# Attention groups in twos: the last score of one group beside the first score of the next

## The chip, the cores and the metric

The kernel runs on one core of one Trainium2 chip. The metric is the device time of one execution in microseconds, the median of several runs. The engines that matter here are TensorE (PE, matrix multiplication), ScalarE (ACT, activations such as the exponential), VectorE (DVE, reductions) and GpSimd (POOL); SyncE (SP) issues the DMAs.

## The reference

One transformer block without learned norm weights, on 2048 rows of 512 numbers:

```python
h = x + _A_ref(_layernorm(x), wqkv, wo)       # S = 2048, D = 512
h2 = h + _B_ref(_layernorm(h), w1, w2)        # F = 1792

def _A_ref(x, wqkv, wo):                      # 32 heads of 16 columns
    q, k, v = ...                             # x @ wqkv, split by head
    scores = jnp.einsum("bhqd,bhkd->bhqk", q, k) * Dh ** -0.5
    p = _softmax(scores, axis=-1)
    return einsum("bhqk,bhkd->bhqd", p, v) (heads joined) @ wo

def _B_ref(x, w1, w2):
    return silu(x @ w1) @ w2
```

## The kernel before, in words

The kernel projects queries, keys and values first (until about 190 us of the span). Then comes attention, with the output projection and the MLP of each block of 512 rows put in as soon as the heads of that block are done.

Attention is cut into 32 items (`ITEMS`). An item is four heads by 512 query rows. Each item is cut into 16 groups (`KC`), one for each 128 keys, so there are 512 groups. A group `g` has four scores, numbered `k` = 0 to 3, one for each head (in the last item, two heads by two chunks of keys). For each score, `scores(g, k)` (L414) does one matmul of the keys with the queries into a PSUM bank (`ps_s`, 128 keys by 512 queries, recorded at L96 as all matmuls) and one exponential on ACT from that bank into an SBUF tile (`pt`, L110). Two groups later, `values(g - LAG)` (L749, `LAG` is 2) multiplies the four `pt` with the values into one bank (`pv`, eight recorded matmuls).

The softmax needs each query's largest score ahead of time, since the negative maximum is part of the operands (extra rows of `qs` and `ks`). So each item's maxima are found some items earlier: `one_max` (L358) calls `maximum` (L259), one matmul of queries with keys into a bank (`ps_m`) and one reduction on DVE (`mx`, L271). There are 64 for each item. `maxima(g)` (L1154) plans how many of them (0 to 3, mostly 3) go into a group. When an item's maxima are complete, `place_max` transposes them and sends them to the operands by DMA.

The operands of a score take 64 rows and those of a maximum 48, so one of each fits on the array at a time, if they lie in different halves of the rows. `HEADS` gives each score number its pair `(a, j)`, and `j` is the half: scores 0 and 2 of a group are in half 1, scores 1 and 3 in half 0 (in the last item 0 and 2 in half 0). `one_max` is called with the other half, `1 - j`, so that the maximum can stand beside the score just issued.

The order on each engine is the order in which the program issues, written out by hand: matmuls, activations, reductions and DMAs are kept in program order. Behind the scores and maxima of a group come the placing of finished maxima, in a few groups the output projection (`output`), and then the values of two groups before.

During attention the eight PSUM banks are given out by

```python
open_banks(ctx, 2, st=4, m0=1, m1=1, pv=1, m2=1)
```

Scores take the four `st` banks in turn, as do the output projections; maxima take `m0`, `m1` and `m2` in turn; `pv` is one bank. A tile in a bank can be written only after the readers of the tile that had the bank before are done.

Three groups (`marks`: 144, 272, 400) begin with an MLP block; the scores of such a group and of the next are issued inside the MLP ahead of time, as those of groups 0 and 1 are beside the last projections. Those groups have no maxima. The last twelve groups (500 to 511) have none either, since all 2048 are found by then.

Of the kernel before, what the change touches and what calls it, by code (L numbers as in the profile page):

```python
# [88 lines left out]
def attention_mlp_kernel(ctx: ExitStack, tc: tile.TileContext, x, wqkv, wo, w1, w2, out):  # L89
# [58 lines left out]
    def bank(name, kind="st", dtype=F32):  # L148
        pool_of = banks[kind]
        if isinstance(pool_of, list):  # L150
            pool_of.append(pool_of.pop(0))
            return pool_of[-1].tile([P, 512], dtype, tag=pool_of[-1].name, name=name)
        return pool_of.tile([P, 512], dtype, tag=kind, name=name)
# [88 lines left out]
    def head(g, k):  # L242

        i, c = divmod(g, KC)
        if i < LAST:
            return *HEADS[k], c
        return c // HALF, k % 2, c % HALF * 2 + k // 2

    def piece_of(i, a):

        return i, a if i == LAST else None
# [7 lines left out]
    def maximum(i, kb, qt, a, j, ps=None):  # L259

        piece = piece_of(i, a)
        n = 1 if i == LAST else 2
        if piece not in mx:
            mx[piece] = small.tile([P, 64], F32, name="mx", bufs=RING + 1)[:, :32 * n].rearrange(
                "p (j a q k) -> p j a q k", j=2, a=n, k=4)
            left[piece] = 32 * n
        if ps is None:
            ps = bank("ps_m", "sm")
        mm(ps, qs[i % RING][64 * j:64 * j + 48, a, qt * P:qt * P + P],
           ks[i % RING][64 * j:64 * j + 48, a, kb * 512:kb * 512 + 512], start=True, stop=True)  # L270
        pin(nc.vector.tensor_reduce(mx[piece][:, j, a % n, qt, kb:kb + 1], ps, axis=AX.X, op=ALU.max))  # L271
        left[piece] -= 1
        return left[piece] == 0

    def finish_max(piece, urgent):

        m4 = mx.pop(piece).rearrange("p j a q k -> p (j a q) k")
        rows = m4.shape[1]
        nm = small.tile([P, 16], F32, name="nm")[:, :rows]
        sign = 1.0  # L280
        if urgent:
            pin(nc.vector.tensor_reduce(nm, m4, axis=AX.X, op=ALU.max, negate=True))  # L282
        else:
            sign = -1.0
            m1, m2 = m4[:, :, :2], m4[:, :, 2:]
            for to, a, b in ((m2, m1, m2), (nm, m2[:, :, 0], m2[:, :, 1])):

                pool("tensor_tensor", to, b, a, ALU.subtract)
                pool("tensor_scalar", to, to, 0.0, None, op0=ALU.max)
                pool("tensor_tensor", to, to, a, ALU.add)  # L290
        ns = small.tile([P, 32], F16, name="ns")[:, :2 * rows]
        high, rest = (ns.rearrange("p (j r a) -> p j r a", j=2, r=2)[:, :, r, :] for r in range(2))
        nm = nm.rearrange("p (j a) -> p j a", j=2)
        pool("tensor_scalar", nm, nm, sign / MX, None, op0=ALU.mult)
        pool("tensor_copy", high, nm)
        pool("tensor_tensor", rest, nm, high, ALU.subtract)
        split[piece] = ns
# [3 lines left out]
    def finish_rest():  # L301
        while unfinished:
            finish_max(unfinished.pop(), True)
# [27 lines left out]
    def soon(steps, fn, *a):  # L331

        agenda.setdefault(at["step"] + steps, []).append((fn, a))
# [11 lines left out]
    def next_item():  # L345
        while at["item"] < ITEMS and not (todo[at["item"], 0] or todo[at["item"], 1]):
            at["item"] += 1
        return at["item"]

    def due_at(piece):  # L350

        g = at["group"]
        if g is None:
            return WAIT + 1
        joint = g + WAIT + (JOINT - g - WAIT) % KC
        return joint - g if joint < start_of(piece) - 2 and joint // KC - 1 not in (-1, *FIRSTS) else WAIT

    def one_max(half=None, ps=None):  # L358

        i = next_item()  # L360
        if i == ITEMS:
            return
        if half is None:
            half = at["half"]
            at["half"] = 1 - half
        if at["blocks"]:

            i = min(range(2), key=lambda n: (todo[n, half] or todo[n, 1 - half] or [(n, KC)])[0][1])
        elif not todo[i, half] and 64 * (i + 2) <= at["ready"] and KC * i - at["next"] > 12:

            i += 1
        half = half if todo[i, half] else 1 - half
        at["done"] += 1
        block = todo[i, half].pop(0)
        piece = piece_of(i, block[3])
        found_all = maximum(*block, ps)

        finish_rest()
        if found_all:
            steps = due_at(piece)  # L380
            g = at["group"]
            if g is None or g + 1 in marks:
                soon(steps, place_max, piece)
                finish_max(piece, g is not None)
                return
            late.setdefault(at["step"] + steps, []).append(piece)
            if steps == WAIT:
                unfinished.append(piece)
                found_at["step"] = at["step"]
            else:  # L390
                finish_max(piece, False)
# [15 lines left out]
    pts, den, pools = {}, {}, []  # L407
# [6 lines left out]
    def scores(g, k, kind="st"):  # L414

        i = g // KC
        a, j, c = head(g, k)
        assert piece_of(i, a) in placed
        ps = bank("ps_s", kind)
        mm(ps, ks[i % RING][64 * j:64 * j + 64, a, c * P:(c + 1) * P], qs[i % RING][64 * j:64 * j + 64, a, :],  # L420
           start=True, stop=True)
        pts[g, k] = pt_tile("pt")
        act("activation", pts[g, k], ps, AF.Exp, scale=qk_f)


    with ExitStack() as pa:
# [289 lines left out]
        for g in range(1, NG // 2):  # L716
            for m, (b, key) in enumerate([(b, 1) for b in range(NB)] + [(b, 0) for b in range(NB)]):
# [3 lines left out]
                n = 8 * g + m - 12  # L721
# [5 lines left out]
                beside = {BESIDE_A1[m]: 6} if g == 1 and m < len(BESIDE_A1) else BESIDE_A  # L727
                if n >= 18:
                    beside = BESIDE_T[n - 18]
# [446 lines left out]
    for g in range(groups):  # L1176
        tick()
        i, c = divmod(g, KC)
        at["group"], at["next"] = None, g
        if g in marks:  # L1180
            finish_block(i // 8 - 1, (g - 2, g - 1))
        if i + RING - 1 < ITEMS and 6 <= c < 14:
            (load_k if c % 2 else load_q)(i + RING - 1, c // 2 - 3)
        if g < DC:
            w = raw_tile()
            dma(w, wo[g * P:(g + 1) * P, :])
            soon(8, split_wo, g, w)
        f, c4 = divmod(g - SPLIT, 4)
        if c4 == 0 and 0 <= f < 2 * FC:
            kind, f = ("w1", "w2")[f % 2], f // 2  # L1190
            soon(4, split_weights, kind, f, load_raw(kind, f))
        if i in FIRSTS:
            b, n = i // 8 - 1, c - OUTPUT
            if c < 4:
                load_rows(b, c)
            if c in first_weights:
                load_weights(*first_weights[c])
            if c in (3, 4):

                split_rows(b, c - 3, slice(0, DC - 1))  # L1200
            if n == 0:
                for t in range(2):
                    split_rows(b, t, slice(DC - 1, DC))
        if i == LAST:
            if c < 4:
                load_rows(NB - 1, c)
            if 5 <= c < 9:

                split_early(c - 5)
            if c == 4:  # L1210
                for f in range(3):
                    load_weights("w1", f)
                load_weights("w2", 0)
        if g == 1:
            dve("memset", pv, 0.0)
        at["group"] = g
        n = maxima(g)

        half = 1 - head(g, g % 2)[1]
        j = next_item()  # L1220
        more = len(todo[j, half]) - len(todo[j, 1 - half]) if j < ITEMS else 0
        beside = range(n)
        if n == 3 and more < 0:
            beside = range(1, 4)
        if n == 2 and more > 0:
            beside = 0, 2
        for m in range(4):
            k = m ^ (g % 2)
            if (g, k) not in pts:
                scores(g, k)  # L1230
            if m in beside:
                one_max(1 - head(g, k)[1])
        if found_at["step"] < at["step"]:
            finish_rest()
        for j in late.pop(at["step"], ()):

            place_max(j)
        if i in FIRSTS and OUTPUT + 1 < c < OUTPUT + 4:

            split_rows(i // 8 - 1, c - OUTPUT)  # L1240
        if i in FIRSTS and c > OUTPUT:
            output(i // 8 - 1, c - OUTPUT - 1)
        if g - LAG >= 0 and not (g in marks or g - 1 in marks):
            values(g - LAG)
# [34 lines left out]
```

## Time and profile before

| | |
|---|---|
| median of 3 runs | 1631.33 us (1630.3 to 1633.35) |
| the profiled execution | 1629.9 us, its span 1628.1 us |
| granted TensorE clock | 0.997 of full speed |
| PE, DVE, ACT busy | 1609.1, 1408.7, 1207.2 us |
| exponentials of scores on ACT | 2048, 1010.5 us |
| reductions of maxima on DVE | 1971 from ps_m, 1232.9 us, and 77 from pv, 52.9 us |

Rows of the timeline have the start, the duration, the engine, the line, the operation, what it writes and reads, and how many instructions are merged; in brackets is the idle time of the engine ahead of it and what ended it. PE durations are modelled: matmuls overlap, so the distance between two starts says more than a duration. The chain of work is followed back from the last instruction, in each step to what released it; "issue" is time in which the engine waited for nothing that the profile shows. A row of the waits has the total idle time in us, how often, and the longest.

### The profile page before, as it was taken

What the parts mean: (1) busy time and instruction counts of PE and PEld (TensorE: products, weight loads), DVE (VectorE), ACT (ScalarE), POOL (GpSimd) and SP (SyncE); (2) the same over time, 40 slices, a digit from 0 to 9 for tenths busy, and PEclk for the clock granted to TensorE, in tenths of its full rate; (3) what the DMA queues carried; (4) which work ended last, traced back from release to release, by engine and by line L of the source; (5) the groups of instructions that cost most, each with busy time, mean ns of one, the idle gap of its engine ahead of it and who ended that gap; (6) DMA issues with size and microseconds to landing.
All of it is one profiled execution on the core that took longest, in us unless ns stands there. A gap on an engine that the chain in (4) does not pass through costs nothing.

```text
span 1628.1 us, 28586 instructions
## 1 busy us (share of the span) xinstructions
PE 1609.1 (99%) x10553; PEld 518.3 (32%) x10553; DVE 1408.7 (87%) x2340; ACT 1207.2 (74%) x2391; POOL 443.7 (27%) x696
## 2 busy tenths in 40 slices
PE   9899999999999999999999999999999999999998
PEld 7566522222223322222223322222223322222254
DVE  7799999999998889999998889999986789998431
ACT  5445599999974249999974249999974179999732
POOL 4323454534524301121225201121126201111100
PEclk9999999999999999999999999999999999999999
DMA  5657343433432211111232211112133211100222
GB/s 194 172 143 220 102 96 113 114 98 107 118 90 69 88 51 32 33 37 46 58 77 86 72 51 33 33 37 53 52 78 95 62 51 34 35 12 22 72 85 71
DMA packets 100952, 125.91 MB, mean 77 GB/s; under 512 B 24144, under 2 KB 61072, under 8 KB 100812
## 3 DMA queue, kind: packets, MB, share of 16 engines
q1 hardware_dynamic: 100812, 124.10, 27.4%
q8 instruction: 82, 1.34, 0.3%
q14 instruction: 58, 0.48, 0.1%
HBM read 93.45 MB, written 24.63 MB: 73 GB/s over the span
## 4 chain that ended last, share of the span: by engine, by line
PE 88%; DVE 6%; ACT 4%; DMA 1%; issue 1%; POOL 0%; SPq 0%; DVEq 0%; ACTq 0%
PE pv L96 30%; PE ps_s L96 22%; PE ps_m L96 9%; PE ps_acc L96 9%; PE ps_w L96 8%; PE ps_qk L96 5%; DVE mx L271 4%; ACT pt L110 3%; PE ps_wo L96 2%; PE ps_v L96 2%; DMA ks<-in_B_w_dram 1%; PE ps_tr L99 1%; DVE st L113 0%; PE ps_n L99 0%; DVE ot L113 0%
## 5 line engine op out<-in xcount | busy, mean ns | idle before, releaser
L271 DVE TENSOR_REDUCE mx<-ps_m 128x1 f32<-128x512 f32 x1971 | 1232.9, 682 | 53.8 <-PE ps_m L96 23.3
L110 ACT ACTIVATE pt<-ps_s 128x512 f32<-128x512 f32 x2048 | 1010.5, 609 | 152.2 <-PE ps_s L96 133.0
L96 PE MATMUL pv<-pt,va 128*17 128x512 f32 x4096 | 537.5, 598 | 0.6
L96 PE MATMUL ps_s<-qs,ks 64*128 64x512 f16 x2048 | 532.5, 379 | 2.3 <-ACT pt L110 0.5
L96 PE MATMUL ps_m<-ks,qs 48*128 48x512 f16 x1971 | 499.3, 380 | 5.5 <-DVE mx L271 5.2
L96 PEld LDWEIGHTS <-ks 64*128 64x128 f16 x2048 | 149.8, 95 | 548.5 <-issue 434.7
L103 POOL TENSOR_TENSOR ri<-rc,minus 128x16 f32<-128x16 f32 x31 | 90.7, 2927 | 261.5 <-DMA rc<-dn 261.5
L96 PE MATMUL ps_acc<-w,gh 128*128 128x512 f16 x672 | 157.2, 380 | 0.0
L96 PEld LDWEIGHTS <-qs 48*128 48x128 f16 x2048 | 119.0, 94 | 65.0 <-issue 54.5
L96 PEld LDWEIGHTS pv<-pt,va 128*17 128x17 f32 x4096 | 68.9, 95 | 215.9 <-issue 203.7
L110 ACT ACTIVATE g<-ps_w,factors 128x512 f32<-128x512 f32 x56 | 38.5, 687 | 127.6 <-PE ps_w L96 123.3
L96 PE MATMUL ps_w<-hth,w 128*128 128x512 f16 (+1 forms) x472 | 132.9, 369 | 0.0
L96 PEld LDWEIGHTS <-w 128*128 128x128 f16 x708 | 66.1, 98 | 87.9 <-issue 20.8
L96 PEld LDWEIGHTS <-gh 128*128 128x128 f16 x672 | 61.1, 98 | 90.9 <-issue 25.0
L271 DVE TENSOR_REDUCE mx<-pv 128x1 f32<-128x512 f32 x77 | 52.9, 687 | 42.6 <-PE ps_m L96 41.2
L103 POOL TENSOR_TENSOR mx<-mx 128x32 f32<-128x32 f32 x40 | 9.6, 241 | 284.9 <-DVE mx L271 283.2
L96 PE MATMUL ps_w<-htl,w 128*128 128x512 f16 (+1 forms) x236 | 83.9, 368 | 0.0
L103 POOL TENSOR_SCALAR nm<-nm 128x16 f32<-128x16 f32 (+1 forms) x53 | 13.5, 254 | 176.2 <-DVE nm L282 148.7
L110 ACT ACTIVATE ks<-ps_qk,qk_s 128x512 f32<-128x512 f32 x30 | 20.7, 688 | 53.2 <-PE ps_qk L96 45.7
L113 DVE SCALAR_TENSOR_TENSOR gh<-g,factors,gh 128x512 f16<-128x512 f32 x14 | 10.5, 752 | 52.1 <-ACT gh L110 52.1
L103 POOL TENSOR_TENSOR sl<-ks,sh 128x512 f16<-128x512 f32 x30 | 34.8, 1161 | 70.4 <-ACT sh L110 57.0
L96 PE MATMUL ps_qk<-xth,wqk_h 128*128 128x512 f32 x128 | 53.6, 419 | 0.4 <-ACT va L110 0.4
(133 smaller groups left out, 1046.5 us busy)
## 6 DMA issues: line engine op xcount, KB each, us to landing
ks<-kd SPq DMA_DIRECT2D x120, 192.0 KB
w<-w1d SPq DMA_DIRECT2D x56, 256.0 KB
w<-w2d SPq DMA_DIRECT2D x56, 256.0 KB
ks<-in_B_w_dram SPq DMA_DIRECT2D x28, 256.0 KB
w<-in_B_w_dram SPq DMA_DIRECT2D x28, 256.0 KB
qs<-qd SPq DMA_DIRECT2D x128, 48.0 KB
kd<-sh SPq DMA_DIRECT2D x16, 256.0 KB
qd<-sh SPq DMA_DIRECT2D x16, 256.0 KB
```

The lines of the kernel that those rows point to most:

```text
L96: tc.keep_in_program_order(nc.tensor.matmul(*a, **k))
L99: tc.keep_in_program_order(nc.tensor.transpose(*a))
L103: tc.keep_in_program_order(getattr(nc.gpsimd, op)(*a, **k))
L110: pin(getattr(nc.scalar, fn)(*a, **k))
L113: pin(getattr(nc.vector, fn)(*a, **k))
L271: pin(nc.vector.tensor_reduce(mx[piece][:, j, a % n, qt, kb:kb + 1], ps, axis=AX.X, op=ALU.max))
```

## The change

Groups are taken in twos. In an even group `g` the loop goes over five scores, the four of `g` and then score 0 of group `g + 1`. In an odd group it goes over the other three, 1, 2 and 3. Before, an odd group took its four in the order 1, 0, 3, 2. Each score may have a maximum behind it, as before; with three maxima in an even group these go behind its first three scores, so that the fourth score (half 0) has the fifth (half 1) as its neighbour. In an odd group each of its three scores has a maximum. The number of maxima planned for each group is the same. The rule that shifted three maxima to the last three scores when the halves were unevenly used up is gone. The values of two groups before still come at the end of each group, so in an even group they now stand behind five scores.

```diff
-        half = 1 - head(g, g % 2)[1]
+        if g % 2:
+            slots = [(g, k) for k in (1, 2, 3)]
+        else:
+            slots = [(g, k) for k in range(4)] + [(g + 1, 0)]
+        half = 1 - head(*slots[0])[1]
         j = next_item()
         more = len(todo[j, half]) - len(todo[j, 1 - half]) if j < ITEMS else 0
-        beside = range(n)
-        if n == 3 and more < 0:
-            beside = range(1, 4)
-        if n == 2 and more > 0:
-            beside = 0, 2
-        for m in range(4):
-            k = m ^ (g % 2)
-            if (g, k) not in pts:
-                scores(g, k)
+        beside = (0, 2) if n == 2 and more > 0 else range(n)
+        for m, slot in enumerate(slots):
+            if slot not in pts:
+                scores(*slot)
             if m in beside:
-                one_max(1 - head(g, k)[1])
+                one_max(1 - head(*slot)[1])
```

## The prediction

> **What bounds the kernel now.** First the head of the page:
>
> ```profile
> span 1628.1 us, 28586 instructions
> PE 1609.1 (99%) x10553; PEld 518.3 (32%) x10553; DVE 1408.7 (87%) x2340; ACT 1207.2 (74%) x2391; POOL 443.7 (27%) x696
> L110 ACT ACTIVATE pt<-ps_s 128x512 f32<-128x512 f32 x2048 | 1010.5, 609 | 152.2 <-PE ps_s L96 133.0
> ```
>
> TensorE (PE) looks like the bound and ScalarE (ACT) like an engine with room. But these are averages over projections, attention and three MLP blocks, so the next view is the table of busy time by stretch, in a stretch that holds attention groups alone:
>
> ```profile
> core 0: us, PE busy (x) PEld busy (x) DVE busy (x) ACT busy (x) POOL busy (x), PEclk, DMA share, GB/s
> 1000.00:1050.00 50.00, 50.00 (x386) 11.35 (x389) 48.04 (x78) 50.00 (x103) 10.86 (x19) 1.00 0.19 48
> ```
>
> There ACT is busy for all of the 50 us, like PE. The timeline of one group, and of ACT over twenty groups, shows how the two stand to one another:
>
> ```profile
> 702.12 0.39 PE L96 MATMUL ps_s<-qs,ks 64*128 64x512 f16 x1
> 702.12 0.60 PE L96 MATMUL ps_m<-ks,qs 48*128 48x512 f16 x2
> 702.35 0.59 PE L96 MATMUL ps_s<-qs,ks 64*128 64x512 f16 x2
> 702.57 0.38 PE L96 MATMUL ps_m<-ks,qs 48*128 48x512 f16 x1
> 702.78 0.38 PE L96 MATMUL ps_s<-qs,ks 64*128 64x512 f16 x1
> 703.09 1.05 PE L96 MATMUL pv<-pt,va 128*17 128x512 f32 x8
> 704.08 0.39 PE L96 MATMUL ps_s<-qs,ks 64*128 64x512 f16 x1
> ...
> 659.79 40.41 ACT L110 ACTIVATE pt<-ps_s 128x512 f32<-128x512 f32 x82
> ```
>
> The group starts at 702.12 with a score and a maximum beside it, and takes four slots: 702.12, 702.35, 702.57 and, for the last score alone, 702.78. That is 0.22 us a slot. The values follow 0.31 after the last score, and the next group starts 0.99 after them. So PE's period is 704.08 - 702.12 = 1.96 us. ACT does 82 exponentials in 40.41 us without a gap; 40.41 / 82 = 0.493 with the drain of the last, about 0.49 each. Four of them take 4 x 0.49 = 1.96 us. **PE and ACT have the same period.** One slot less on PE finds ACT already full.
>
> There is a third limit, four PSUM banks for scores. The end of attention, where no maxima are left, shows it bare. First the timeline, then the chain of work there:
>
> ```profile
> 1524.27 0.61 PE L96 MATMUL ps_s<-qs,ks 64*128 64x512 f16 x4
> 1524.69 4.03 ACT L110 ACTIVATE pt<-ps_s 128x512 f32<-128x512 f32 x8 [0.39 <-PE ps_s L96]
> 1524.81 0.13 PEld L96 LDWEIGHTS pv<-pt,va 128*17 128x17 f32 x8 [0.42 <-issue]
> 1524.81 1.05 PE L96 MATMUL pv<-pt,va 128*17 128x512 f32 x8
> 1525.79 1.39 PE L96 MATMUL ps_s<-qs,ks 64*128 64x512 f16 x4
> 1527.11 1.05 PE L96 MATMUL pv<-pt,va 128*17 128x512 f32 x8
> 1528.10 0.66 PE L99 MATMUL ps_o<-ident,o_t 128*128 128x128 f32 x4
> 1529.11 1.57 ACT L110 ACTIVATE pt<-ps_s 128x512 f32<-128x512 f32 x3 [0.39 <-PE ps_s L96]
> ...
> 1524.71 2.06 ACT pt L110 x4
> 1526.77 0.04 issue
> 1526.81 0.37 PE ps_s L96
> 1527.18 0.98 PE pv L96 x8
> ```
>
> At 1524.27 four scores go in two slots (0.61 for all) and values follow 0.54 later: two neighbouring scores of unlike halves do share a slot, which is what the change counts on. The next four scores, from 1525.79, take 1.39 instead: each waits until the exponential four places earlier has emptied its bank. The chain says so: four exponentials end at 1526.77, and 0.04 later, at 1526.81, the last score starts. Then the values stand behind it at 1527.11, 0.30 on, and the next PE work at 1528.10.
>
> **The change part by part.** What it removes: the slot in which the last score of an even group stands alone. Two groups have eight score slots in the period before (3.92 us) and seven after. On PE alone that is worth 0.22 us for two groups.
>
> What it adds: the first score of the odd group is issued ahead of the even group's values instead of behind them, as the fifth score in a row. Call the eight scores of two groups s0 to s7, with exponentials e0 to e7. With four banks, s4 uses the bank of s0 and waits for the end of e0. Until now the values, 1.3 us from the last score to the next group, lay between s3 and s4, and e0 was over long before:
>
> ```profile
> PE ps_s L96 <- ACT pt L110: 0.5, 3, 0.2
> L110 ACT ACTIVATE pt<-ps_s x2048: 570/603/710, 191.6 to 1534.4; 128x512 f32<-128x512 f32 x187
> ```
>
> The first row is the whole kernel's wait of scores for exponentials, 0.5 us; the second is one exponential's duration, least, median and most.
>
> When does s4 start? e0 starts 0.42 after s0 (1524.27 to 1524.69) if ACT isn't behind, lasts 0.60, and a score follows 0.04 to 0.05 after that. So s4 starts 0.42 + 0.60 + 0.05 = 1.07 after s0, where its slot beside s3 is at 0.66 (702.12 to 702.78). PE stands still for 0.41. Queued behind s4 on PE are the eight matmuls of the values and everything later, since its matmuls start in order; ACT has e1 to e4 in hand meanwhile.
>
> From s4 on: 0.30 to the values, 0.98 to 0.99 to s5 (1526.81 to 1528.10 in all, 1.29). Then the odd group: s5, s6, s7, each with a maximum, are two slot steps (0.44 to 0.45), 0.31 to the values, 0.98 to 0.99 to the next s0; together 1.74. The cycle s0, e0, s4, values, s5 to s7, values, s0 is 1.07 + 1.29 + 1.74 = **4.10 us for two groups**, against 3.92 now. (To more digits the same steps give 4.095.)
>
> Does anything else end later than this cycle? ACT needs 8 x 0.49 = 3.92, so it now idles for 0.175 ahead of each e0, and e0 does start 0.42 after s0. s5, s6 and s7 need e1, e2 and e3, which end 0.49 apart at 1.51, 2.00 and 2.49 after s0, while s5 starts at 2.36, s6 at 2.58 and s7 at 2.80: no wait. VectorE has six maxima in two groups, and 78 instructions at 48.04 us are 0.62 each, 3.7 us: below 4.10. With three banks of its own, the fourth maximum (2.36) comes long after the first one's reduction. The slots beside which maxima stand are the same in number, and the planner's counts don't depend on the order; that the rule for uneven halves is dropped costs at most a few slots of 0.22, next to nothing. The DMA issues of a group are where they were, ahead of its scores. Transposes of finished maxima come behind s4 in an even group, where they lengthen the stretch as they do now.
>
> How often? 2048 / 4 = 512 groups, 256 pairs. The first pair and the three pairs behind an MLP block have their scores issued ahead: 4 pairs less. The last 12 groups have no maxima:
>
> ```profile
> L96 PE MATMUL ps_m<-ks,qs x1971: 372/377/582, 38.9 to 1508.2; 48*128 48x512 f16 x198
> ```
>
> In those s5 and s6 share a slot as well, the cycle is 4.10 - 0.22 = 3.88, below ACT's 3.92, and nothing changes: 6 pairs less. That leaves 246 pairs. Groups with two maxima (beside the placing of a finished maximum, and just ahead of the last twelve) have the same cycle, as s7 still has a slot of its own. Nine pairs hold output projections of the block before, and there s4 waits in the same way.
>
> The sum: 246 x 0.175 = 43 us. The profiled execution took 1629.9 us (span 1628.1 and 1.8 around it), so it would take 1673; the three runs have their median at 1631.33, 1.4 above it, so **1674 us**.
>
> A rule of the Trainium skill speaks against the change. TensorEngine Tiling (Array Packing), section PSUM Bottleneck, says that tiling makes TensorE faster but not the emptying of PSUM, which may then be the bottleneck. By that rule alone the time would stay at 1631; the 50.00 us of ACT in 50 above agree with it, and the wait for a bank goes beyond it.
>
> **The rivals.** *Slower as forecast, but not by this size.* The unknown is e0's duration in the new order. The ends of the row are 0.57 and 0.71: 4.065 and 4.205 for two groups, 246 x 0.145 = 36 and 246 x 0.285 = 70 us, or 1667 and 1701. I take 0.60, the median, since 0.71 occurs where ACT is behind (its start is then early, its end set by the one ahead), and here it idles ahead of e0. The forecast and this spread together: 0.91.
>
> *No change.* The bank comes free early enough for ACT to stay full: the cycle would have to be 0.175 shorter, 3.92. It would be if a bank could be written some 0.2 us ahead of the end of its exponential. Against it are the rows 1526.77 and 1526.81, where the score starts only after that end. 1631 us, chance 0.04.
>
> By the price of another page of the Trainium skill it would be this case: ScalarE: Activation LUTs, section What ACT_TABLE_LOAD costs, gives 186 ns + 0.833 ns per element, less 93 ns where they overlap, for 512 elements 520 ns as an estimate. Eight would be 4.16 us, more than the cycle of 4.10, before and after alike. The trace has 0.49 instead, so ACT isn't long enough to hide the cycle.
>
> *Faster, on the other side.* The slot saved on PE is the whole effect, s4 doesn't hold PE up, and ACT turns out to have some room: it decides if exponentials can follow one another faster than 0.49. The nearest row is the 1.57 us for three, (1.57 - 0.60) / 2 = 0.485; eight are 3.88, a gain of 0.04 for two groups, 246 x 0.04 = 10 us, 1621. The full slot, 246 x 0.22 = 54 us and 1577, would need 0.4625 for each, which no row has. Chance 0.05. That s3 and s4 don't share a slot isn't a case of its own: s4 comes 0.41 late anyway.
>
> **How the numbers follow.** The likeliest case gives 1674. Its own range is 1660 to 1692: below, a cycle of 4.04 or a third of the pairs without the wait; above, e0 at 0.67. The two other cases have 0.09 together and the tail above some 0.05, so this range holds 8 times in 10 and needn't reach to them. 0.2% of the time is 3.3 us, about what a measurement of this kernel can tell from no change. Faster by more: 0.05; within: 0.04; slower: 0.91.
>
> **What would show it.** In the profile after: in a stretch of groups ACT is no longer at 50 of 50 us but at 48 (3.92 / 4.10), and PE, with the same work in more time, has gaps ahead of ps_s released by ACT pt, some 246 of 0.4 us; the chain there runs ps_s, ACT pt of one, ps_s, pv, where it was PE alone; two groups take 4.10. It is wrong if ACT stays at 50.00, if the fifth score starts 0.66 after the first, or if two groups take 3.9 or less.

## The result and the profile after

The changed kernel took 1675.46 us (median of 4 runs, 1674.17 to 1676.54) against 1631.16 us before (4 runs, 1630.3 to 1633.35): a ratio of 1.0269, 95% interval 1.0251 to 1.0287. The forecast was 1674, slower. Its profiled execution has a span of 1672.3 us, 44.2 more than before.

The head of the page, with the group of the exponentials, and the busy times of the stretch from 1000 to 1050 us (columns as in the prediction):

```profile
span 1672.3 us, 28634 instructions
PE 1644.6 (98%) x10553; PEld 497.5 (30%) x10553; DVE 1390.8 (83%) x2340; ACT 1229.1 (74%) x2391; POOL 442.5 (26%) x696
L110 ACT ACTIVATE pt<-ps_s 128x512 f32<-128x512 f32 x2048 | 1032.3, 626 | 172.8 <-PE ps_s L96 126.7
1000.00:1050.00 50.00, 49.75 (x369) 9.58 (x363) 44.93 (x75) 49.11 (x99) 7.09 (x14) 1.00 0.11 27
```

The work is the same (2048 exponentials, 10553 matmuls). In 50 us there are now 99 ACT instructions instead of 103 and 369 matmuls instead of 386. Yet PE is "busy" for 49.75 of 50 us. Busy time doesn't show the loss; the distances between starts in the timeline do (rows that the reading doesn't need are left out, here and below):

```profile
1000.69 0.39 PE L96 MATMUL ps_s<-qs,ks 64*128 64x512 f16 x1
1000.69 0.60 PE L96 MATMUL ps_m<-ks,qs 48*128 48x512 f16 x2
1000.92 0.59 PE L96 MATMUL ps_s<-qs,ks 64*128 64x512 f16 x2
1001.34 0.37 PE L96 MATMUL ps_m<-ks,qs 48*128 48x512 f16 x1
1001.56 0.57 PE L96 MATMUL ps_s<-qs,ks 64*128 64x512 f16 x2
1002.06 1.05 PE L96 MATMUL pv<-pt,va 128*17 128x512 f32 x8
1003.04 0.39 PE L96 MATMUL ps_s<-qs,ks 64*128 64x512 f16 x1
1003.80 1.05 PE L96 MATMUL pv<-pt,va 128*17 128x512 f32 x8
1004.79 0.39 PE L96 MATMUL ps_s<-qs,ks 64*128 64x512 f16 x1
```

Two groups go from 1000.69 to 1004.79: 4.10 us. The even group has its five scores (1, 2 and 2 in the rows). The last row of scores ends at 1001.56 + 0.57 = 1002.13, so the fifth, 0.37 long, starts at 1001.76: 1.07 after the first, as worked out. The values follow 0.30 later, s5 at 1003.04, and the odd group takes 1.75.

One thing there wasn't forecast: the third maximum starts at 1001.34, 0.65 after the group, where it was 0.45 before, and so the fourth score at 1001.56 comes 0.87 after instead of 0.66. It waits for VectorE, which is still at the three reductions of the odd group before, to free one of the three banks. Two exponentials, the last of the pair before and e0, and the last of those reductions, each by itself:

```profile
1000.36 0.67 ACT L110 ACTIVATE pt<-ps_s 128x512 f32<-128x512 f32 x1
1001.11 0.60 ACT L110 ACTIVATE pt<-ps_s 128x512 f32<-128x512 f32 x1
1000.61 0.68 DVE L271 TENSOR_REDUCE mx<-ps_m 128x1 f32<-128x512 f32 x1
```

e0 ends at 1001.71 and the fifth score starts 0.05 later; the reduction ends at 1001.29 and the third maximum starts 0.05 later. So there are two waits ahead of the values, and which one sets the period isn't settled by this profile. That is what the experiments are for.

Over all 2048 score starts of the two profiles: 199 pairs of groups are 0.175 to 0.20 us longer, 35.9 us together; 15, with a maximum placed, are longer by some 0.12, 1.8 us; 14 by 0.27 to 0.49, 5.4 us (six of them place a maximum, three hold an MLP block, two output projections); the other 27 add 1.6. In sum 44.7 us.

### The profile page after: what moved, and what is told of

Same layout as the page of the kernel before. It is cut to its first block, busy times and chain, and to the rows that moved or that the text cites. A ratio compares the mean times of both kernels' runs of the same rounds, so it can differ in the third digit from the quotient of the medians.

```text
span 1672.3 us, 28634 instructions
## 1 busy us (share of the span) xinstructions
PE 1644.6 (98%) x10553; PEld 497.5 (30%) x10553; DVE 1390.8 (83%) x2340; ACT 1229.1 (74%) x2391; POOL 442.5 (26%) x696
## 4 chain that ended last, share of the span: by engine, by line
PE 91%; DVE 4%; ACT 3%; DMA 1%; issue 0%; POOL 0%; SPq 0%; DVEq 0%; ACTq 0%
PE pv L96 31%; PE ps_s L96 22%; PE ps_m L96 12%; PE ps_acc L96 9%; PE ps_w L96 8%; PE ps_qk L96 5%; DVE mx L271 3%; ACT pt L110 3%; PE ps_wo L96 2%; PE ps_v L96 2%; DMA ks<-in_B_w_dram 1%; PE ps_tr L99 1%; DVE ot L113 0%; DVE st L113 0%; PE ps_n L99 0%
## 5 line engine op out<-in xcount | busy, mean ns | idle before, releaser
L271 DVE TENSOR_REDUCE mx<-ps_m 128x1 f32<-128x512 f32 x1971 | 1214.6, 681 | 112.8 <-PE ps_m L96 111.3
L110 ACT ACTIVATE pt<-ps_s 128x512 f32<-128x512 f32 x2048 | 1032.3, 626 | 172.8 <-PE ps_s L96 126.7
L96 PE MATMUL ps_s<-qs,ks 64*128 64x512 f16 x2048 | 560.9, 379 | 7.7 <-ACT pt L110 6.1
L96 PE MATMUL ps_m<-ks,qs 48*128 48x512 f16 x1971 | 528.2, 380 | 6.4 <-DVE mx L271 6.1
L96 PEld LDWEIGHTS <-ks 64*128 64x128 f16 x2048 | 130.5, 94 | 562.3 <-issue 500.4
L110 ACT ACTIVATE ks<-ps_qk,qk_s 128x512 f32<-128x512 f32 x30 | 20.6, 688 | 51.6 <-PE ps_qk L96 44.3
```

The costliest lines, as they stand in the source:

```text
L96: tc.keep_in_program_order(nc.tensor.matmul(*a, **k))
L110: pin(getattr(nc.scalar, fn)(*a, **k))
```

## The experiments

Theory A: s4 waits for the bank of e0 with the values behind it. Theory B: six maxima stand in a shorter stretch, and the wait is for VectorE.

**The fifth score behind the values** (`fifth_behind`), five rounds:

```diff
             if m in beside:
                 one_max(1 - head(*slot)[1])
+            if m == (2 if g % 2 else 3) and g - LAG >= 0 and not (g in marks or g - 1 in marks):
+                values(g - LAG)
...
-        if g - LAG >= 0 and not (g in marks or g - 1 in marks):
-            values(g - LAG)
```

> The fifth score is issued behind the even group's values instead of ahead of them; the taking in twos and the order of the scores stay. It no longer shares a slot with the fourth score, so two groups have eight slots again. If the loss comes from the fifth score waiting for e0's bank with the values queued behind it (theory A), the wait is gone, two groups take 3.92 us and the time is about 1631 us. If it comes from the uneven division itself, five exponentials and then three, or from the maxima standing closer together in the odd group (theory B), two groups still take about 4.10 us and the time is about 1675 us.

1675.45 us, ratio 1.0273 (1.0259 to 1.0287), as slow as the change. Taken by itself this speaks for B. The edit also puts the values ahead of the placing of a finished maximum in the same group; so do values_mid and values_mid_in_before. The timeline of two groups, the odd one first:

```profile
1000.66 0.39 PE L96 MATMUL ps_s<-qs,ks 64*128 64x512 f16 x2
1000.89 0.38 PE L96 MATMUL ps_m<-ks,qs 48*128 48x512 f16 x2
1001.30 3.68 DVE L271 TENSOR_REDUCE mx<-ps_m 128x1 f32<-128x512 f32 x6 [0.41 <-PE ps_m L96]
1002.62 0.39 PE L96 MATMUL ps_s<-qs,ks 64*128 64x512 f16 x1
1003.24 0.37 PE L96 MATMUL ps_m<-ks,qs 48*128 48x512 f16 x1
1003.46 0.38 PE L96 MATMUL ps_s<-qs,ks 64*128 64x512 f16 x1
1003.76 1.05 PE L96 MATMUL pv<-pt,va 128*17 128x512 f32 x8
1004.75 0.39 PE L96 MATMUL ps_s<-qs,ks 64*128 64x512 f16 x2
```

No score in this stretch waits for an exponential: s4 and s5 start together at 1000.66. But the odd group's maxima now begin one slot later (1000.89), VectorE is at work without a gap for six reductions, and the even group's third maximum comes at 1003.24, 0.62 after the group. The fourth score and the values stand behind it; 1000.66 to 1004.75 is 4.09 us. This would fit two cycles, one through e0 and one through VectorE, of which this edit took away the first and lengthened the second by a slot; the short reductions below test it.

**The values inside the group** (`values_mid`), and the same in the kernel before (`values_mid_in_before`), five rounds each. The edit is as above, with `m == 1 - g % 2` in the one and `m == 1` in the other.

> The values are issued inside the group, behind the second score and its maximum in an even group and behind the first in an odd one, so that fourth and fifth score still share a slot, but e0 is over by then (they come 1.73 us after s0 instead of 0.66). Theory A: no score waits long for its bank, PE needs only 7 slots and two values, 3.70 us for two groups, and ACT sets 8 x 0.49 = 3.92: 1622 to 1631 us, the part below 1631 from places where PE has extra work (transposes of maxima, output projections). Theory B: about 1675 us. If ACT is no floor (the rival on the fast side), 3.70 us for two groups and about 1577 us.

> The kernel before with the values behind the second score of each group, eight slots for two groups: the control for the run with the values inside the group. Theory A: PE 3.92 and ACT 3.92 us for two groups, 1629 to 1633 us; what values_mid has below this is the slot saved. Theory B has nothing to say here: 1631 us.

values_mid: 1705.32 us, ratio 1.0455 (1.0441 to 1.0469). Both theories missed it. The timeline:

```profile
1002.16 0.39 PE L96 MATMUL ps_s<-qs,ks 64*128 64x512 f16 x1
...
1004.35 0.38 PE L96 MATMUL ps_m<-ks,qs 48*128 48x512 f16 x1
1004.36 3.18 DVE L271 TENSOR_REDUCE mx<-ps_m 128x1 f32<-128x512 f32 x5 [0.28 <-PE ps_m L96]
1004.70 0.37 PE L96 MATMUL ps_s<-qs,ks 64*128 64x512 f16 x1
1005.10 0.37 PE L96 MATMUL ps_m<-ks,qs 48*128 48x512 f16 x1
1005.41 1.05 PE L96 MATMUL pv<-pt,va 128*17 128x512 f32 x8
1006.39 0.39 PE L96 MATMUL ps_s<-qs,ks 64*128 64x512 f16 x1
```

The group starts at 1004.35; its second maximum, in its slot at 0.22, starts at 1005.10, 0.75 after, with the values right behind it. (Its second score is late too, at 1004.70, 0.35 after: it needs a bank that an exponential has just left.) Four maxima (the odd group's last two, the even group's first two) stand close together there, on three banks. Two groups take 4.23 us (1002.16 to 1006.39).

values_mid_in_before: 1637.04 us, ratio 1.0034 (1.0021 to 1.0048), 4 us above what was expected. The median of two groups is 3.91, close to the 3.92 expected; seven pairs in which a maximum is placed are longer by more than 0.5 each. Why isn't shown; in these the placing now stands behind the values.

**Short exponentials** (`short_exp_before`, `short_exp_after`, `short_exp_values_mid`), three rounds. These kernels leave out the exponentials of 384 of the 512 queries of a tile. Tiles for `pt` are kept in a ring and filled once, so that the columns that are left out hold numbers:

```diff
-        act("activation", pts[g, k], ps, AF.Exp, scale=qk_f)
+        c = 512 if full[0] else 128
+        act("activation", pts[g, k][:, :c], ps[:, :c], AF.Exp, scale=qk_f)
```

(`full` holds for the first use of a tile after an MLP block has written it.)

> The kernel before with exponentials over 128 of the 512 queries (the other columns of the tile keep a constant, so attention isn't computed for them); matmuls, maxima and values as before. ACT has room then: an exponential takes perhaps 0.28 us instead of 0.60 (an estimate, between a quarter of it and the whole). PE alone sets the period, 3.92 us for two groups: 1620 to 1631 us.

> The changed kernel with the same short exponentials. Theory A: the cycle s0, e0, s4, values, s5 to s7, values is 0.42 + 0.28 + 0.05 + 1.29 + 1.74 = 3.78 us for two groups, so the change is now a gain of 0.14 x 246 = 34 us against short_exp_before (between 14 and 50 us for exponentials of 0.36 to 0.22). Theory B in the form of uneven maxima on VectorE: still slower than short_exp_before by some 40 us.

> The kernel with the values inside the group, with the same short exponentials: neither ACT nor a bank holds PE up, and two groups take 7 slots and two values, 3.70 us: 0.22 x 246 = 54 us less than short_exp_before. If fourth and fifth score don't truly share a slot, no less than short_exp_before. VectorE, six maxima of about 0.61 us, needs 3.64.

short_exp_before: 1628.24 us. ACT falls to half, and two groups still take 3.92:

```profile
1000.00:1050.00 50.00, 50.00 (x386) 11.34 (x386) 48.06 (x78) 24.03 (x103) 12.30 (x25) 1.00 0.20 49
```

So PE sets 3.92 by itself, as the prediction read it. short_exp_after: 1627.97 us. The loss is gone, but instead of a gain of 34 us there is none. Its timeline:

```profile
1000.20 0.39 PE L96 MATMUL ps_s<-qs,ks 64*128 64x512 f16 x1
1001.94 0.39 PE L96 MATMUL ps_s<-qs,ks 64*128 64x512 f16 x1
1002.36 0.71 ACT L110 ACTIVATE pt<-ps_s 128x128 f32<-128x128 f32 x3 [1.03 <-PE ps_m L96]
1002.60 0.37 PE L96 MATMUL ps_m<-ks,qs 48*128 48x512 f16 x1
1002.69 0.50 PE L96 MATMUL ps_s<-qs,ks 64*128 64x512 f16 x2
1003.12 1.05 PE L96 MATMUL pv<-pt,va 128*17 128x512 f32 x8
1003.23 0.45 ACT L110 ACTIVATE pt<-ps_s 128x128 f32<-128x128 f32 x2 [0.15 <-PE ps_s L96]
1004.11 0.39 PE L96 MATMUL ps_s<-qs,ks 64*128 64x512 f16 x1
```

e0 starts at 1002.36 and lasts 0.28, so its bank is free at 0.70 after the group. The third maximum still starts at 1002.60, 0.66 after, and the score behind it and the values follow: 1000.20 to 1004.11 is 3.91 us. This is the cycle through VectorE alone, 0.19 shorter than the one through e0. short_exp_values_mid took 1700.03 us: nearly as slow as values_mid and far from the gain of 54 us expected, so there it wasn't ACT.

**Short reductions** (`short_max_after`, `short_max_fifth_behind`, `short_max_values_mid`, and the control `short_max_before`), three rounds. Here a maximum is that of 128 of its 512 columns:

```diff
-        pin(nc.vector.tensor_reduce(mx[...], ps, axis=AX.X, op=ALU.max))
+        pin(nc.vector.tensor_reduce(mx[...], ps[:, :128], axis=AX.X, op=ALU.max))
```

> The changed kernel with reductions over 128 of the 512 columns of each maximum (the maxima are those of a part of the keys, so the shifts differ; matmuls, exponentials and values as before). VectorE has room then and gives its three banks back early. Theory A (the fifth score waits for e0's bank and the values stand behind it): that cycle has no maximum in it, so two groups still take 4.10 us: about 1674 us. Theory B (six maxima in a shorter stretch, whose third waits for VectorE to free a bank): the wait is gone and the time falls to 1631 us or below.

> The kernel before with the short reductions: the control for the three runs with them. short_max_after took 1659 us with two groups still at 4.10 us, short_max_fifth_behind 1619 us with 3.917. Theory A: ACT sets 3.92 us for two groups here too, and what the short reductions save lies in the projections and the MLP blocks, about 12 us in all three kernels: 1619 us, so that short_max_after is 40 us behind its own control. Theory B (short reductions save mostly in the changed kernel's groups): 1630 us.

short_max_after: 1659.25 us, between the two times expected, so the kernel before was run with short reductions too. Against the 1614.11 us of this control it is 45.1 us, the whole loss (44.3 in the medians of the two kernels). The timeline with the short reductions:

```profile
999.80 0.39 PE L96 MATMUL ps_s<-qs,ks 64*128 64x512 f16 x1
1000.25 0.38 PE L96 MATMUL ps_m<-ks,qs 48*128 48x512 f16 x1
1000.26 0.73 DVE L271 TENSOR_REDUCE mx<-ps_m 128x1 f32<-128x128 f32 x3 [1.01 <-PE ps_m L96]
1000.47 0.78 PE L96 MATMUL ps_s<-qs,ks 64*128 64x512 f16 x2
1001.18 1.05 PE L96 MATMUL pv<-pt,va 128*17 128x512 f32 x8
1002.16 0.39 PE L96 MATMUL ps_s<-qs,ks 64*128 64x512 f16 x1
1003.90 0.39 PE L96 MATMUL ps_s<-qs,ks 64*128 64x512 f16 x1
```

VectorE idles 1.01 us ahead of the reductions. The third maximum (1000.25) and the fourth score (1000.47) are at 0.45 and 0.67 after the group, as before the change. The fifth still starts at 1000.88 (1000.47 + 0.78 - 0.37), 1.08 after, and two groups take 4.10 (999.80 to 1003.90). B is out as the cause of the loss; what is left is the wait for e0. The control has 3.920 for two groups. It gained 17 us, more than the 12 expected; the 15 by which its profile is shorter lie in the MLP blocks with maxima beside them (about 8 us), in pairs that place a maximum (5) and ahead of the attention loop (2).

> The fifth score behind the values, with the short reductions. In fifth_behind the third maximum of an even group started 0.655 after the group instead of 0.447, as the last reduction of the odd group ended only then. Theory A with a second cycle through VectorE (third maximum, fourth score, values, the odd group's maxima one slot later, their three reductions, third maximum: 3.9 + 0.22): both cycles are gone, 3.92 us for two groups, about 1631 us. If the division into five and three exponentials costs by itself: about 1675 us still.

short_max_fifth_behind: 1619.06 us, with 3.917 for two groups (median). With both waits gone the loss is gone, 12 us below the time expected, since the short reductions save elsewhere too. It is 5 us above the control, mostly in pairs that place a maximum (15 of them, 4.11 to 4.18 against 3.86 to 3.96).

> The values inside the group, with the short reductions. In values_mid the second maximum waited 0.53 us for a bank ahead of the values (0.756 instead of 0.222). Without this wait nothing holds PE up: 3.70 us on PE, 3.92 on ACT for two groups, so ACT sets 1622 to 1631 us. If the place of the values inside the group costs by itself: still near 1700 us.

1626.35 us: 79 below values_mid, so the wait of the maximum was the cause there. It is 12 above the control, with 3.98 for two groups (median), so the change gains nothing in this order either; where these 12 come from was not followed up.

**Both short** (`short_both_after`, `short_both_values_mid`), three rounds: the two edits together.

> The changed kernel with short exponentials and short reductions (neither attention nor the maxima computed in full). In short_exp_after two groups took 3.906 us, with the third maximum 0.43 late; the cycle through e0 alone is, with the measured 0.277 us of a short exponential, 0.42 + 0.28 + 0.05 + 1.29 + 1.74 = 3.78. Theory A with the second cycle through VectorE: 3.78, so 0.14 x 246 = 34 us below short_exp_before, about 1594 us. If the third maximum waited for something else than VectorE: 1628 us as in short_exp_after.

1580.83 us, ratio 0.9693 (0.9677 to 0.9709) to the kernel before. That is 13 below the time expected, which left out what short reductions save elsewhere; 33.3 below short_max_before, 47.4 below short_exp_before. The timeline:

```profile
999.89 0.39 PE L96 MATMUL ps_s<-qs,ks 64*128 64x512 f16 x1
1001.63 0.39 PE L96 MATMUL ps_s<-qs,ks 64*128 64x512 f16 x1
1002.06 1.10 ACT L110 ACTIVATE pt<-ps_s 128x128 f32<-128x128 f32 x5 [1.03 <-PE ps_m L96]
1002.30 0.46 PE L96 MATMUL ps_s<-qs,ks 64*128 64x512 f16 x2
1002.69 1.05 PE L96 MATMUL pv<-pt,va 128*17 128x512 f32 x8
1003.67 0.39 PE L96 MATMUL ps_s<-qs,ks 64*128 64x512 f16 x1
```

999.89 to 1003.67 is 3.78 us, the sum that the cycle through e0 gives with 0.28 for e0. From 4.10 to 3.78 is 0.32, which is what e0 is shorter (0.60 to 0.28). So the period follows e0's duration one for one, and below 3.92 the change gains: with exponentials and reductions that leave room, the same edit is worth some 33 us (an estimate, against short_max_before, which also takes 3.92 for two groups; the kernel before with both short wasn't run).

> The values inside the group, with short exponentials and short reductions (neither attention nor the maxima computed in full). No bank, neither ACT nor VectorE should hold PE up: seven slots and two values, 3.70 us for two groups, 0.22 x 246 = 54 us below the 1628 us of short_exp_before, about 1574 us. If fourth and fifth score don't share a slot, 3.92 and 1628 us.

1595.96 us, 22 above the time expected, with 3.83 for two groups (median): fourth and fifth score do share a slot (below 3.92). The 0.13 above the expected 3.70 is the second maximum of a group:

```profile
1004.00 0.60 PE L96 MATMUL ps_m<-ks,qs 48*128 48x512 f16 x2
1004.44 0.38 PE L96 MATMUL ps_m<-ks,qs 48*128 48x512 f16 x1
1004.45 1.05 DVE L271 TENSOR_REDUCE mx<-ps_m 128x1 f32<-128x128 f32 x4 [1.01 <-PE ps_m L96]
1004.80 0.37 PE L96 MATMUL ps_m<-ks,qs 48*128 48x512 f16 x1
```

The group's first maximum is the one at 1004.44, the second the one at 1004.80, 0.36 later instead of 0.22. It needs the bank of the maximum at 1004.00, whose reduction starts only at 1004.45 and, short as it is (0.29), ends at 1004.74, 0.06 before.

No version with the whole work came out below the kernel before. short_max_values_mid and short_both_values_mid have the same order and differ in the exponentials alone: 3.98 against 3.83 for two groups. That fits the 3.92 of ACT as a floor, with 0.06 left over.

## Why the prediction was right, step by step

The term that carries it, the cycle s0, e0, s4, values, s5 to s7, values, was worked out as 4.10 (4.095) and measured as 4.10. Its parts hold one by one: s4 1.07 after s0, 1.29 to s5, 1.74 for the odd group. short_max_after shows that this wait alone makes the loss, short_both_after that it follows e0.

The count was 246 pairs at 0.175, 43 us; it was 199 pairs at 0.18, 15 at some 0.12 and 7 us in the others, 44.7 in all. That the two sums lie so close is partly luck: fewer pairs than counted lose 0.18, and 14 others lose up to 0.49. The 26 pairs in which a maximum is placed and that took 3.98 before take 4.10 (15) or 4.13 to 4.14 (11) now: some or all of the 0.06 that they were longer is hidden behind s4's wait.

One step failed, the one on VectorE. It asked whether the *fourth* maximum waits for a bank and found that it doesn't. The next even group's *third* one does: the odd group is only three slots long, 1.74 us, and three reductions take longer. This wait, 0.2 us, cost nothing in the ordinary pairs, as the fourth score was still ahead of the later s4. But it is a cycle of its own of 3.91 us (short_exp_after), just under ACT's 3.92, and it would have been next in line had e0's been shorter. It is also why the two edits meant to free the change of e0's wait (fifth_behind, values_mid) stayed slow.

What the profile would show was half right. ACT did fall below 50 of 50, but to 49.11, not 48. The sum 8 x 0.49 counts e0 like one in a row, but after an idle ACT it takes its whole 0.60, so eight take 0.60 + 7 x 0.49 = 4.03 and ACT idles 0.07 in 4.10: in the rows above from 1001.03 to 1001.11. The cycle had e0 at 0.60, so the time doesn't change. And the gaps ahead of ps_s that ACT releases, expected 246 times, aren't in the view of the waits:

```profile
PE ps_s L96 <- ACT pt L110: 6.1, 24, 0.6
```

The modelled durations of the matmuls ahead, the late maximum and the fourth score, cover them. The chain of work, for the same reason, still shows PE nearly alone in these groups (ACT has 3.0% of it from 1000 to 1020 us).

On the rivals: ACT's floor fits the runs (3.98 and 3.83 above), and short_exp_before shows that PE has the same one. The estimate of 520 ns from the figures of the Trainium skill (ScalarE: Activation LUTs, section What ACT_TABLE_LOAD costs) would have hidden the cycle; the 4.10 us agree with the 0.49 us of the trace and not with it. The Trainium skill's rule that the emptying of PSUM may become the bottleneck (TensorEngine Tiling (Array Packing), section PSUM Bottleneck) agrees as far as it goes: the wait for a bank is what held the change up. By that rule alone the time would have stayed at 1631; that it rose by 44 us is the work queued behind the wait.

## What to carry to other kernels

When work is issued earlier in an in-order queue, look for the buffer that it needs at the new place, and count everything queued behind it: here a slot of 0.22 us was saved, and a wait of 0.41 us put ahead of the values for it. Follow every ring of buffers once around the whole period, wrapping into the next one, and not just the first user; cycles of nearly the same length hide one another, and taking away the longest shows the next. And where durations are modelled, read distances between starts: PE was 49.75 of 50 us busy while two groups took 4.10 instead of 3.92.

## What was not expected of the hardware

In short_exp_after the fifth score, which waits for e0 only, seems to start ahead of the fourth, which stands before it in the program. e0 starts at 1002.36 and takes 0.28, and a score starts at 1002.69, 0.05 after it ends; the third maximum starts at 1002.60, and the other score of that row (1002.69 0.50 x2) starts at 1002.82, 0.22 after that maximum, whose half of the rows the fourth score shares. So it looks as if two matmuls in different halves of the array's rows can start out of program order when the earlier one waits; the prediction took them to start in order. Which record is which score is inferred from these distances; the trace doesn't name them. The fourth exponential fits the inference: ACT is idle 0.15 and starts it at 1003.23, 0.41 after the score at 1002.82, the distance that a score and its exponential have elsewhere (0.42 for e0), and not after the one at 1002.69.
